# Transposing x of two batches by DMA in a fused attention and feed-forward kernel, with a new order of its steps

## The chip, the cores and the metric

The kernel runs on one core of one Trainium2 chip. A core has five engines that run side by side and wait for each other through semaphores: TensorE (PE in the profile; its weight loads are shown apart as PEld), VectorE (DVE), ScalarE (ACT), GpSimd (POOL) and SyncE (SP). SP does no arithmetic here; it starts DMA transfers, and so does POOL. The transfers of both run on the core's 16 DMA engines. The metric is the device time of the whole program in microseconds, the median of repeated runs.

## The reference

Two parts follow each other. The first is causal attention in a sliding window of 64 positions, for 8 batches of 8 heads, 576 positions and a head size of 64. The second is a feed-forward layer over all 4,608 tokens: 512 to 2,048 features, an activation h - tanh(h), and 2,048 back to 512.

```python
scores = scale * np.matmul(q, k.transpose(0, 1, 3, 2))
mask = (rel >= 0) & (rel < window)                 # rel = query position - key position, window = 64
attn = softmax(np.where(mask, scores, -1e9))
x = np.matmul(attn, v)                             # to (tokens, heads * head_dim) = (4608, 512)
h = x @ w_in                                       # 512 x 2048
out = (h - np.tanh(h)) @ w_out                     # 2048 x 512
```

## The kernel before

All matrix products are bf16 with float32 sums. The kernel is written as small Python functions, one for each kind of step, and a script (the string PLAN, line 537, played at line 621) that names the steps in the order in which they are issued. Each engine runs its own instructions in this order and waits where an operand is not ready or a buffer not free; nothing is reordered at run time. A step is written `kind.arguments`, and a last letter names the engine that does it: a ScalarE, v VectorE, p GpSimd. So the script is both a program and a schedule, and a step moved in it moves in the queue of every engine that it uses.

Attention works by pairs of heads, g = 4 * batch + pair (0 to 31), mostly two pairs at a time. The keys of the window are taken in blocks of 128 for 64 queries, nine query windows for each batch. The steps of a pair of pairs are:

- loads on POOL's queue: `qr` and `lr` bring 128 tokens of q or k of a batch (five pieces each), `LV` brings v in five pieces; for batches 0 to 2 `lk`, `lq` bring k and q of one pair in another layout, and `ck`, `cq` copy these into the order that TensorE transposes (`Fp`, `Ep`, with the copies `Fc`, `Ec` out of PSUM). From batch 3 on, `tk` and `tq` transpose k and q with DMA transposes on SP's queue (lines 171 and 179); `tz` copies the last 64 queries.
- `S` (or `Rp` for batches 0 to 2): scores on TensorE into PSUM; `Sx` (`Rx`): exp on ScalarE; `M`: the mask as a product on VectorE; `Z`, `za`, `zb`: copies of v between the two halves of the partitions.
- `PP`: probabilities times v on TensorE (line 348), with the sums of the rows as a 65th column; `DR` and three `DN` on VectorE: reciprocals, and x in token order into the tile xs (two buffers, by batch).
- x must then be turned so that features lie on partitions. `Xp` does it by TensorE (line 397, 128x128 transposes against an identity into PSUM) and `Xc` copies it into the tile xT; `Y` does it by DMA transposes on SP's queue (line 416), straight from xs to xT. In the kernel before, batches 0 to 3 go by `Xp`, batches 4 to 7 by `Y`.

The feed-forward layer works by chunks c of 512 tokens, nine in all, while a batch has 576, so a batch fills one chunk and the beginning of the next. xT has three buffers, by chunk.

- `H.c.m`: the first layer, 128 of the 2,048 hidden features (m from 0 to 15), four matmuls of 512 columns (line 431); `Hp.c.m.half` is the same in two halves (line 508), where half h needs only that half of x (half 0 comes from pairs 0 and 1 of the batch, half 1 from pairs 2 and 3).
- `A`: tanh on ScalarE (line 439) from PSUM; `G`: h - tanh(h) on VectorE (line 445) into gT. From chunk 2 on the sums of `H` alternate between two PSUM banks, so `H` of an m waits for `G` of the m that had the bank before.
- `W.c.s.part`: the second layer for 128 tokens, four matmuls of 512 columns (line 474), all in PSUM bank 2 for most chunks; `O.c.s`: the copy out of PSUM on ScalarE or VectorE and the output DMA on SP.

A buffer in use is a wait in the queue of whoever wants to write it. `LV` of batch b needs the `PP` steps of batch b - 2, and `qr` and `lr` of batch b need the DMA transposes `tq` and `tk` that read the same piece of batch b - 2. Such a wait on POOL or SP holds everything behind it in that queue.

Of the kernel before, what the change touches and what calls it, by code (L numbers as in the profile page):

```python
# [650 lines left out]
```

## Time and profile before

The time before is 307.63 us, the median of three runs (307.45 to 307.67). The profiled execution has a span of 305.2 us from its first to its last instruction; no time of its own is shown beside that, and the 2.4 us between the span and the median lie before and after it.

| | busy us | share of the span | instructions |
|---|---|---|---|
| TensorE, matmuls | 297.8 | 98% | 2599 |
| TensorE, weight loads (beside matmuls) | 149.4 | 49% | 2632 |
| VectorE | 176.2 | 58% | 316 |
| ScalarE | 157.5 | 52% | 265 |
| GpSimd (mostly issuing loads) | 103.7 | 34% | 141 |

The views used below are: the page (busy shares, the span in 40 slices, the chain of work that ended last), the groups of instructions by line and shape, the waits of an engine, the instructions in order of time, and the DMA issues with their times to landing. Within a row of the time view, the first number is the start, the second the length, and a bracket gives the idle time before it and who ended it. A matmul's length includes its way through the pipeline, so the cost of a matmul in a stream is read from one start to the next, not from its length.

### The profile page before, as it was taken

What the parts mean: (1) busy time and instruction counts of PE and PEld (TensorE: products, weight loads), DVE (VectorE), ACT (ScalarE), POOL (GpSimd) and SP (SyncE); (2) the same over time, 40 slices, a digit from 0 to 9 for tenths busy, and PEclk for the clock granted to TensorE, in tenths of its full rate; (3) what the DMA queues carried; (4) which work ended last, traced back from release to release, by engine and by line L of the source; (5) the groups of instructions that cost most, each with busy time, mean ns of one, the idle gap of its engine ahead of it and who ended that gap; (6) DMA issues with size and microseconds to landing.
All of it is one profiled execution on the core that took longest, in us unless ns stands there. A gap on an engine that the chain in (4) does not pass through costs nothing.

```text
span 305.2 us, 6469 instructions
## 1 busy us (share of the span) xinstructions
PE 297.8 (98%) x2599; PEld 149.4 (49%) x2632; DVE 176.2 (58%) x316; ACT 157.5 (52%) x265; POOL 103.7 (34%) x141
## 2 busy tenths in 40 slices
PE   8999999999999999999999999999999999999995
...
DMA  9999999995999999949999999560143010001112
GB/s 155 159 195 193 195 207 180 159 205 102 102 143 127 173 125 181 182 108 131 164 177 127 135 173 142 95 143 35 37 76 74 0 69 37 34 34 37 52 51 104
DMA packets 132878, 36.77 MB, mean 120 GB/s; under 512 B 119920, under 2 KB 127344, under 8 KB 132848
## 3 DMA queue, kind: packets, MB, share of 16 engines
q0 software_dynamic: 92752, 18.06, 85.3%
...
## 4 chain that ended last, share of the span: by engine, by line
PE 87%; DVE 5%; ACT 3%; issue 2%; POOL 2%; DVEq 0%; ACTq 0%; POOLq 0%
PE ps L474 38%; PE ps L431 30%; PE ps L508 6%; PE ps L348 3%; PE ps L304 2%; DVE gT L445 2%; PE ps L397 1%; ACT th L439 1%; PE ps L286 1%; PE ps L467 1%; DVE pt L323 1%; PE ps L260 1%; PE ps L281 1%; PE ps L227 1%; POOL qall L110 1%
## 5 line engine op out<-in xcount | busy, mean ns | idle before, releaser
L445 DVE TENSOR_TENSOR gT<-ps,th 128x512 bf16<-128x512 f32 x144 | 97.2, 687 | 85.3 <-ACT th L439 84.6
L474 PE MATMUL ps<-w_out_sb,gT 128*128 128x512 bf16 x527 | 131.5, 380 | 2.2 <-issue 0.8
L439 ACT ACTIVATE th<-ps 128x512 f32<-128x512 f32 x144 | 84.7, 599 | 93.0 <-PE ps L431 79.7
L431 PE MATMUL ps<-xT,wi 128*128 128x512 bf16 x496 | 120.7, 380 | 0.1
L474 PEld LDWEIGHTS <-gT 128*128 128x128 bf16 x560 | 53.3, 98 | 61.4
L431 PEld LDWEIGHTS <-wi 128*128 128x128 bf16 x496 | 47.0, 98 | 54.3
L145 POOL DMA_DIRECT2D vw<-in_v_dram x35 | 30.0, 872 | 36.1 <-PE ps L348 33.5
L90 ACT ACTIVATE ysb<-ps 128x512 f32<-128x512 f32 (+1 forms) x24 | 14.2, 593 | 30.9 <-PE ps L474 30.2
L166 POOL DMA_DIRECT2D qall<-in_q_dram x25 | 21.7, 881 | 24.1 <-DMA qw<-qall 21.4
L166 POOL DMA_DIRECT2D kall<-in_k_dram x25 | 21.7, 875 | 10.4 <-DMA kw<-kall 4.8
L314 ACT ACTIVATE pt<-ps 128x1024 bf16<-128x1024 f32 (+1 forms) x30 | 23.3, 816 | 3.5 <-PE ps L304 3.2
L323 DVE TENSOR_TENSOR pt<-pt,ps 128x1152 bf16<-128x1152 bf16 x28 | 20.5, 749 | 5.1 <-ACT pt L314 3.2
L508 PE MATMUL ps<-xT,wi 128*128 128x512 bf16 x80 | 20.8, 380 | 0.0
L92 DVE COPY ysb<-ps 128x512 f32<-128x512 f32 (+1 forms) x11 | 7.1, 650 | 20.5 <-PE ps L467 13.2
L368 DVE TENSOR_TENSOR xs<-ps,rcp 128x384 bf16<-128x384 f32 x28 | 15.2, 550 | 0.3
L318 ACT ACTIVATE pt<-ps 128x640 bf16<-128x640 f32 (+1 forms) x24 | 14.7, 659 | 0.8 <-PE ps L286 0.8
L348 PEld LDWEIGHTS <-pt 128*64 128x64 bf16 x504 | 9.4, 112 | 6.3 <-DVE pt L323 2.1
L90 ACT ACTIVATE kt<-ps 128x576 bf16<-128x576 bf16 x10 | 6.5, 647 | 10.8 <-PE ps L256 6.8
L227 PE MATMUL ps<-warm 128*128 128x512 bf16 (+1 forms) x35 | 10.6, 435 | 1.1 <-DVE warm L207 1.1
L508 PEld LDWEIGHTS <-wi 128*128 128x128 bf16 x80 | 7.4, 98 | 8.5 <-issue 0.4
L348 PE MATMUL ps<-vw,pt 128*64 128x65 bf16 x504 | 11.0, 197 | 0.3 <-DVE pt L323 0.2
L365 DVE TENSOR_TENSOR xs<-ps,rcp 128x384 bf16<-128x384 f32 x14 | 7.7, 550 | 0.1
...
## 6 DMA issues: line engine op xcount, KB each, us to landing
...
vw<-in_v_dram POOLq DMA_DIRECT2D x28, 128.0 KB, 6.6
qall<-in_q_dram POOLq DMA_DIRECT2D x20, 128.0 KB, 7.5
kall<-in_k_dram POOLq DMA_DIRECT2D x20, 128.0 KB, 6.8
...
```

The source lines that it names most:

```text
L90: nc.scalar.activation(o, i, ACT.Copy)
L145: nc.gpsimd.dma_start(out=w[:, 2 * i + 1, :, 0:D] if i < NF else w[64:128, 2 * i, :, 0:D], in_=v[b, :, 128 * i:128 * i + n].rearrange("h p ...
L166: nc.gpsimd.dma_start(out=token_rows(b, n)[0:c, i], in_=(q if n == "q" else k)[b, :, 128 * i:128 * i + c].rearrange("h p d -> p h d"))
L314: nc.scalar.activation(o, sp, ACT.Exp, scale=scale)
L323: nc.vector.tensor_tensor(p, p, mask.unsqueeze(1).to_broadcast([128, 2 * NJ, 64]), ALU.mult)
L348: nc.tensor.matmul(ps[r, bank, 65 * i:65 * i + 65], PT[(g + r2) % NPT][:, j, r], vw[b % 2][:, j, p0 + r2 + NP * h, :], start=True, stop=True)
L368: nc.vector.tensor_tensor(xs[b % 2][:, p0 // 2, 0:6, n // 2, :], ov[:, :, 0:D], sums[g][:, n].to_broadcast([128, 6, D]), ALU.mult)
L431: nc.tensor.matmul(hp, w_in_tile(ki, m), chunk_tile(c)[:, n.start // 64:n.stop // 64, ki % 2, 64 * (ki // 2):64 * (ki // 2) + 64], start=( ...
L439: nc.scalar.activation(th[:, n], hp, ACT.Tanh)
L445: nc.vector.tensor_tensor(gT[c][:, m, columns(s)], hp, th, ALU.subtract)
L474: nc.tensor.matmul(yp, gT[c][:, m, s * 128:(s + 1) * 128], w_out_sb[:, m, :], start=n == 1 and i == 0, stop=n == 4 and i == 3)
L508: nc.tensor.matmul(hp, w_in_tile(half + 2 * i, m), chunk_tile(c)[:, :, half, 64 * i:64 * i + 64], start=n == 1 and i == 0, stop=n == 2 and ...
```

## The change

Nothing is changed in the functions; the script gets a new text from step `Ep.8` on, just before chunk 0's last first-layer steps H.0.14, H.0.13 and H.0.15. The 16 steps `Xp` and `Xc` of batches 2 and 3 are gone (8 each, 36 TensorE transposes), and in their place stand `Y.2.0`, `Y.2.1`, `Y.3.0` and `Y.3.1`, eight more DMA transposes on SP's queue (each batch's half lies in two chunks, so each step issues two). All other steps stay, in a new order, and some get another engine or PSUM bank: `ck.9` and `cq.11` from ScalarE and VectorE to GpSimd, `zb.1.3` from GpSimd to ScalarE, `za.1.2` from VectorE to ScalarE and `za.1.3` the other way, `tz.3` and `tz.7` to GpSimd, and several output copies between ScalarE and VectorE. The attention of batches 3 to 7 stands earlier in the script. In the diff below the first part of both texts is shown, to the attention of batch 4.

```diff
@@ the script PLAN, from line 553 on
-    cq.8.v G.0.9 G.0.10 Rp.7.1.3 A.0.11 wo.2 Fc.8.7.a G.0.11 Rp.7.0.5 H.0.12 lk.9.p Rx.7.0.5 A.0.12 Ep.8.1
-    Rx.7.1.3 cq.9.v H.0.14 M.4 wo.3 zb.1.3.p G.0.12 Ec.8.1.a PP.4 wo.1 A.0.14 H.0.15 mk DR.4 DN.4.1 G.0.14
-    A.0.15 H.0.13 DN.4.0 za.1.3.a W.0.0.0 Rp.8.0.3 G.0.15 A.0.13 Rp.8.1.5 DN.4.2 zb.1.2.a za.1.2.v Rx.8.1.5
-    W.0.1.0 M.7 qr.3.3 LV.2.3 lk.11.p PP.6 Rx.8.0.3 Xp.1.0.1.3 W.0.0.2 G.0.13 Xp.1.0.0.4 DR.6 Xc.1.0.1.3.a
-    DN.6.2 DN.6.0 W.0.1.2 DN.6.1 Xp.1.1.0.5 lk.10.p ck.9.a Xc.1.0.0.4.a Fp.9.3 Xc.1.1.0.5.a Xp.1.1.1.4
-    lr.3.2 lq.10.p lq.11.p LV.2.2 Hp.1.0.0 Ep.9.7 Xc.1.1.1.4.v Ec.9.7.a Fc.9.3.a Hp.1.0.1 W.0.1.3 W.0.0.3
-    qr.3.4 LV.2.0 Rp.9.1.5 Rp.9.0.3 LV.2.1 W.0.0.1 O.0.0.a M.8 LV.2.4 W.0.1.1 lr.3.1 lr.3.4 A.1.0 tq.3.4
-    G.1.0 O.0.1.a Rx.9.1.5 Rx.9.0.3 ck.11.a M.9 ck.10.a W.0.2.1 W.0.2.0 W.0.2.3 W.0.2.2 W.0.3.2 qr.3.1
-    O.0.2.a Fp.11.5 cq.10.v W.0.3.1 W.0.3.3 Hp.1.1.1 W.0.3.0 Fp.10.7 Ep.10.3 Hp.1.1.0 O.0.3.v Ec.10.3.v
-    Hp.1.2.1 Hp.1.2.0 Fc.10.7.a A.1.1 A.1.2 Rp.10.1.3 G.1.1 cq.11.v G.1.2 Fc.11.5.a H.1.3 Ep.11.6 tk.3.2
-    A.1.3 Rx.10.1.3 H.1.4 A.1.4 G.1.3 Ec.11.6.a H.1.5 A.1.5 qr.3.0 Z.2 H.1.6 qr.3.2 PP.8 G.1.5 Rp.11.0.3
-    A.1.6 tk.3.1 tq.3.3 lr.3.0 H.1.8 Rx.11.0.3 G.1.4 G.1.6 DR.8 H.1.7 DN.8.2 A.1.8 A.1.7 H.1.9 tq.3.1 G.1.8
-    H.1.11 G.1.7 A.1.9 tk.3.4 H.1.10 lr.3.3 A.1.11 A.1.10 DN.8.1 G.1.9 Rp.11.1.3 Rx.11.1.3 Rp.10.0.6 tq.3.2
-    G.1.11 DN.8.0 G.1.10 Rx.10.0.6 H.1.12 tq.3.0 M.10 H.1.14 A.1.12 M.11 H.1.13 Xp.2.0.1.3 Xp.2.0.0.4 G.1.12
-    A.1.13 A.1.14 Xc.2.0.1.3.a PP.10 H.1.15 LV.4.1 LV.3.1 A.1.15 Xc.2.0.0.4.a LV.3.3 G.1.13 LV.3.2 LV.3.0
-    DR.10 DN.10.1 DN.10.0 tk.3.0 DN.10.2 tk.3.3 LV.3.4 LV.4.0 G.1.14 lr.4.2 qr.4.0 lr.4.1 lr.4.0 qr.5.3
-    LV.4.2 W.1.0.1 W.1.0.2 Xp.2.1.1.6 W.1.0.0 G.1.15 qr.4.1 lr.4.4 Xp.2.1.0.5 Xc.2.1.0.5.a W.1.0.3
-    Xc.2.1.1.6.v qr.4.3 lr.4.3 H.2.3 Hp.2.0.0 Hp.2.0.1 tk.4.4 O.1.0.a A.2.3 LV.4.3 qr.4.4 LV.4.4 A.2.0
-    W.1.1.2 G.2.3 Hp.2.1.0 tz.3.a Hp.2.1.1 W.1.1.3 G.2.0 qr.4.2 qr.5.4 lr.5.2 H.2.2 A.2.1 G.2.1 S.12 A.2.2
-    G.2.2 H.2.5 Sx.12.2 Sx.12.0 W.1.1.1 Z.3 W.1.1.0 A.2.5 Sx.12.1 O.1.1.a tk.4.1 tq.4.0 M.12 tk.4.0 H.2.4
-    M.13 tk.4.3 tq.4.4 G.2.5 A.2.4 PP.12 W.1.2.3 H.2.7 lr.6.4 lr.5.4 DR.12 DN.12.2 G.2.4 tq.4.3 tk.4.2
-    tq.4.1 lr.6.3 DN.12.0 A.2.7 lr.5.3 lr.5.1 lr.5.0 tq.4.2 DN.12.1 H.2.6 G.2.7 qr.5.2 S.14 H.2.9 A.2.6
-    Sx.14.2 Sx.14.1 A.2.9 tk.5.4 Sx.14.0 G.2.6 G.2.9 M.14 M.15 qr.6.0 W.1.2.0 H.2.8 W.1.2.1 W.1.2.2
-    Xp.3.0.1.3 A.2.8 G.2.8 tq.5.3 H.2.11 O.1.2.v PP.14 DR.14 H.2.10 A.2.11 A.2.10 Xc.3.0.1.3.v G.2.10
-    Xp.3.0.0.4 W.1.3.2 G.2.11 tq.5.4 W.1.3.3 H.2.12 A.2.12 H.2.13 Z.4 A.2.13 W.1.3.1 G.2.12 G.2.13 H.2.14
-    W.1.3.0 H.2.15 DN.14.2 O.1.3.a DN.14.1 A.2.15 A.2.14 DN.14.0 Xp.3.1.0.6 W.2.0.1 Xp.3.1.1.7 W.2.0.0
-    G.2.14 W.2.0.2 Xc.3.1.1.7.v Xc.3.0.0.4.a Xc.3.1.0.6.a G.2.15 qr.5.0 Hp.3.0.0 W.2.0.3 Hp.3.1.1 Hp.3.1.0
-    O.2.0.a A.3.1 W.2.1.1 Hp.3.0.1 W.2.1.2 G.3.1 tz.4.v A.3.0 S.16 Sx.16.2 W.2.1.3 Sx.16.1 G.3.0 H.3.3
-    W.2.1.0 M.17 Sx.16.0 M.16 H.3.2 A.3.3 PP.16 G.3.3 O.2.1.a A.3.2 tk.5.2 qr.5.1 qr.6.4 H.3.5 LV.5.3
-    W.2.2.1 DR.16 A.3.5 tk.5.1 DN.16.2 tq.5.2 G.3.2 DN.16.1 H.3.4 DN.16.0 Y.4.0 A.3.4 S.18 G.3.5 W.2.2.0
...
+    cq.8.v G.0.9 G.0.10 Rp.7.1.3 A.0.11 wo.2 Fc.8.7.a G.0.11 Rp.7.0.5 H.0.12 lk.9.p Rx.7.0.5 A.0.12 Ep.8.7
+    Rx.7.1.3 cq.9.v H.0.14 M.4 G.0.12 Ec.8.7.a A.0.14 H.0.13 wo.3 H.0.15 M.7 G.0.14 LV.2.0 wo.1 qr.3.1
+    lk.10.p ck.9.p qr.3.0 lq.11.p lk.11.p lq.10.p LV.2.3 qr.3.2 lr.3.0 qr.3.4 cq.11.p LV.2.1 LV.2.2 LV.2.4
+    PP.4 Rp.8.0.3 W.0.0.0 A.0.13 A.0.15 za.1.3.v zb.1.3.a Rx.8.0.3 za.1.2.a Rp.8.1.3 Rx.8.1.3 zb.1.2.a DR.4
+    G.0.15 DN.4.0 DN.4.2 DN.4.1 W.0.1.0 Ep.9.4 G.0.13 Xp.1.0.0.3 PP.6 Xp.1.0.1.1 W.0.1.2 Xc.1.0.0.3.v
+    Xc.1.0.1.1.a DR.6 DN.6.2 DN.6.1 W.0.0.2 Fp.9.6 Hp.1.0.0 DN.6.0 Xp.1.1.0.5 Xp.1.1.1.3 Xc.1.1.1.3.v
+    Ec.9.4.v Xc.1.1.0.5.a Fc.9.6.a W.0.0.3 W.0.1.3 Rp.9.1.6 Rp.9.0.3 Hp.1.0.1 W.0.0.1 W.0.1.1 O.0.0.a
+    Rx.9.1.6 A.1.0 O.0.1.a tk.3.0 tq.3.1 lr.3.2 lr.3.3 lr.3.4 tk.3.2 ck.10.a cq.10.a W.0.2.3 W.0.2.1 W.0.2.2
+    W.0.2.0 W.0.3.0 G.1.0 ck.11.v M.8 lr.3.1 tk.3.3 tq.3.2 tk.3.4 tk.3.1 tq.3.0 qr.3.3 LV.3.3 tq.3.3 LV.3.1
+    LV.3.0 LV.3.2 Ep.11.6 Ep.10.1 Ec.10.1.v O.0.2.a Rx.9.0.3 M.9 W.0.3.1 W.0.3.2 Fp.11.5 Fp.10.4 W.0.3.3
+    Hp.1.1.1 Hp.1.1.0 O.0.3.a Fc.10.4.v Ec.11.6.v Fc.11.5.a A.1.1 G.1.1 H.1.3 Hp.1.2.1 Rp.11.1.3 Rp.10.0.5
+    Hp.1.2.0 H.1.4 A.1.3 Rx.10.0.5 Rx.11.1.3 A.1.2 G.1.3 Z.2 G.1.2 H.1.6 Rp.10.1.3 PP.8 A.1.4 A.1.6
+    Rx.10.1.3 G.1.4 H.1.5 H.1.7 A.1.5 A.1.7 DR.8 G.1.6 M.10 G.1.5 DN.8.0 G.1.7 H.1.9 A.1.9 G.1.9 H.1.8 A.1.8
+    G.1.8 DN.8.1 Rp.11.0.3 H.1.10 A.1.10 Rx.11.0.3 H.1.12 H.1.11 A.1.12 A.1.11 G.1.10 DN.8.2 M.11 H.1.13
+    PP.10 G.1.12 G.1.11 H.1.15 A.1.13 tq.3.4 tz.3.p qr.5.4 qr.4.4 LV.3.4 lr.4.4 lr.4.0 lr.4.2 lr.4.3 qr.4.1
+    qr.4.2 lr.4.1 qr.5.0 qr.5.2 qr.4.0 qr.4.3 Y.2.0 H.1.14 A.1.15 A.1.14 G.1.13 DR.10 DN.10.2 DN.10.0
+    DN.10.1 G.1.14 G.1.15 mk Y.2.1 W.1.0.0 W.1.0.2 W.1.0.1 W.1.0.3 S.12 Hp.2.0.0 Sx.12.1 Sx.12.2 Sx.12.0
+    O.1.0.v W.1.1.1 W.1.1.2 Hp.2.0.1 Hp.2.1.1 Hp.2.1.0 W.1.1.3 A.2.0 A.2.1 Z.3 M.12 G.2.0 G.2.1 M.13 H.2.2
+    H.2.3 PP.12 A.2.2 G.2.2 A.2.3 H.2.4 A.2.4 G.2.3 DR.12 DN.12.0 G.2.4 DN.12.1 DN.12.2 W.1.1.0 H.2.5 tq.4.4
+    tk.4.2 Y.3.0 tk.4.4 tq.4.2 tk.4.3 tk.4.0 H.2.6 S.14 O.1.1.a A.2.5 A.2.6 G.2.6 G.2.5 W.1.2.1 W.1.2.2
+    H.2.10 tk.4.1 tq.4.3 tq.4.0 tq.4.1 H.2.11 W.1.2.3 W.1.2.0 Sx.14.1 Sx.14.2 tz.4.a Sx.14.0 A.2.11 A.2.10
+    G.2.11 G.2.10 M.14 H.2.13 H.2.8 O.1.2.v M.15 A.2.13 A.2.8 G.2.13 G.2.8 W.1.3.3 W.1.3.1 H.2.7 H.2.12
+    A.2.12 A.2.7 W.1.3.2 W.1.3.0 PP.14 G.2.12 G.2.7 DR.14 DN.14.0 DN.14.2 DN.14.1 O.1.3.a H.2.15 A.2.15
+    Y.3.1 qr.5.1 LV.4.3 LV.4.0 qr.5.3 qr.6.1 LV.4.4 LV.4.1 LV.5.0 lr.5.1 lr.6.3 lr.5.4 lr.5.2 LV.4.2 LV.5.1
+    lr.6.1 qr.6.0 LV.5.2 lr.5.3 lr.5.0 qr.6.3 LV.5.4 qr.6.4 tk.5.2 tk.5.1 tk.5.4 tq.5.4 G.2.15 W.2.0.0
+    H.2.14 H.2.9 A.2.14 A.2.9 S.16 G.2.9 W.2.0.1 W.2.0.2 G.2.14 W.2.0.3 Sx.16.2 Sx.16.0 Sx.16.1 M.17 O.2.0.v
+    M.16 Hp.3.0.1 Hp.3.0.0 Hp.3.1.1 W.2.1.0 Hp.3.1.0 A.3.0 G.3.0 A.3.1 G.3.1 W.2.1.2 W.2.1.3 H.3.2 W.2.1.1
+    H.3.3 A.3.2 G.3.2 O.2.1.a A.3.3 G.3.3 H.3.4 A.3.4 W.2.2.3 W.2.2.2 H.3.7 W.2.2.0 G.3.4 Z.4 PP.16 DR.16
+    A.3.7 H.3.6 W.2.2.1 G.3.7 DN.16.0 DN.16.1 DN.16.2 A.3.6 O.2.2.a G.3.6 H.3.5 S.18 A.3.5 G.3.5 H.3.8 A.3.8
+    Sx.18.2 Sx.18.0 Sx.18.1 G.3.8 M.18 M.19 W.2.3.2 H.3.9 W.2.3.1 W.2.3.0 A.3.9 G.3.9 H.3.10 PP.18 H.3.11
...
+    W.8.2.0 W.8.2.2 W.8.2.3 W.8.2.1 W.8.3.3 O.8.2.v O.9.0.a W.8.3.0 W.8.3.1 O.8.3.v"""
```

73 lines of the change are left out of this document (35 added, 38 removed).

## The prediction

> **What bounds the kernel now.** I read the page first (busy shares, slices, chain), then the waits of TensorE, then the groups by line, and last the time view around the steps that move.
>
> ```profile
> span 305.2 us, 6469 instructions
> PE 297.8 (98%) x2599; PEld 149.4 (49%) x2632; DVE 176.2 (58%) x316; ACT 157.5 (52%) x265; POOL 103.7 (34%) x141
> PE   8999999999999999999999999999999999999995
> DMA  9999999995999999949999999560143010001112
> PE 87%; DVE 5%; ACT 3%; issue 2%; POOL 2%; DVEq 0%; ACTq 0%; POOLq 0%
> ```
>
> TensorE is busy in every slice from the second to the last but one, and 87% of the chain that ended last is its own work. The DMA engines are full until about slice 28 (214 us).
>
> ```profile
> PE ps L227 <- DVE warm L207: 1.1, 1, 1.1
> PE ps L474 <- issue: 0.8, 5, 0.2
> PE ps L348 <- DVE pt L323: 0.2, 1, 0.2
> PEld L348 <- DVE pt L323: 2.1, 5, 0.5
> ```
>
> The matmuls themselves hardly wait; the weight loads ahead of the probabilities-times-v products (PP) wait 2.1 us, of which most is hidden under the matmul still running. So the end is set by how much TensorE has to do plus what it waits, and every term below is a sum on TensorE's queue.
>
> **What is removed.** 36 of 72 transposes (Xp), and their copies out of PSUM (Xc).
>
> ```profile
> L397 PE MATMUL ps<-ident,xs 128*128 128x128 bf16 x72 | 6.3, 220 | 0.0
> 44.39 0.45 PE L397 MATMUL ps<-ident,xs 128*128 128x128 bf16 x5
> 44.68 0.38 PE L474 MATMUL ps<-w_out_sb,gT 128*128 128x512 bf16 x1
> L90 ACT ACTIVATE xT<-ps 128x512 bf16<-128x512 bf16 x7 | 4.1, 600 | 2.2 <-PE ps L397 2.2
> ```
>
> Five transposes start at 44.39 and the next matmul at 44.68: 0.29 / 5 = 58 ns each, so 36 x 58 ns = 2.1 us leave TensorE. The 220 ns in the group's row is the length through the pipeline and is not what one costs in a stream. "TensorE: Matmul & The Clock Gate" in the Trainium skill (Part 4: PE-mode transpose) gives about 275 ns for such a transpose in one kernel; by that figure 9.9 us would leave, an estimate from that page, and the row above contradicts it. The copies are worth nothing directly: ScalarE is 52% and VectorE 58% busy; at the full 0.6 us each in a stretch where one of them is the bound, they are counted there.
>
> Old waits go as well, because the steps around them move. Their bounds are 0.2 (the matmuls' own row) and 2.1 us (the weight loads' row); I take 0.6, nearer the matmuls' row, since a weight load runs ahead of its matmul.
>
> **What is added: waits in the new order.** TensorE blocks are counted from these rows: four matmuls of H or W 0.86 us, a PP 0.70, a score block S 0.79 (from 85.75 to 86.54), a transpose of q or k (Ep) 0.25 (60.30 to 60.55), two score groups Rp issued together 0.37 (71.48 to 71.85), alone about half of it and a change of shape, 0.3.
>
> ```profile
> 245.73 0.86 PE ps L474 x4
> 100.23 0.70 PE ps L348 x35
> 85.75 0.22 PE L299 MATMUL ps<-q,kw 128*128 128x64 bf16 x2
> 86.54 1.04 PE L431 MATMUL ps<-xT,wi 128*128 128x512 bf16 x4
> 60.30 0.42 PE L260 MATMUL ps<-ident,qb 96*128 96x96 bf16 x6
> 60.55 1.46 PE L508 MATMUL ps<-xT,wi 128*128 128x512 bf16 x6
> 71.48 0.43 PE L286 MATMUL ps<-qp,kt 64*128 64x64 bf16 x18
> 71.85 2.77 PE L431 MATMUL ps<-xT,wi 128*128 128x512 bf16 x12
> ```
>
> (1) Around PP.6. In the new order ScalarE has, from the end of H.0.15 to PP.6, a tanh, zb.1.3, an exp, za.1.2, an exp and zb.1.2, and PP.6 needs the last.
>
> ```profile
> 41.08 0.64 ACT L90 ACTIVATE vw<-vw 64x520 bf16<-64x520 bf16 x1
> 41.62 0.57 ACT L439 ACTIVATE th<-ps 128x512 f32<-128x512 f32 x1
> 42.90 1.19 ACT L318 ACTIVATE pt<-ps 128x512 bf16<-128x512 f32 x2
> ```
>
> That is 0.6 + 3 x 0.64 + 2 x 0.6 and 0.2 to start, 3.9 us. TensorE has PP.4, two Rp, two W, Ep.9 and an Xp of four: 0.70 + 0.6 + 1.72 + 0.25 + 0.23 = 3.5; the second Rp waits for the first's exp and hides some of this. So it waits about +0.4. The pads mk (two memsets) and the output copies that changed engine cost nothing while the 0.86 us blocks between their producer and user cover them; without that cover each would cost its 0.3 to 0.7 us once.
>
> (2) From PP.8 to PP.10.
>
> ```profile
> 66.00:75.00 9.00, 8.94 (x106) 4.72 (x105) 8.55 (x16) 6.21 (x11) 0.00 (x0) 1.00 0.93 130
> 100.00:110.00 10.00, 9.95 (x86) 5.08 (x86) 6.19 (x13) 3.93 (x7) 5.42 (x7) 1.00 1.27 147
> 110.00:120.00 10.00, 9.79 (x82) 5.02 (x83) 4.71 (x9) 5.76 (x11) 4.51 (x6) 1.00 2.31 158
> 66.11 0.76 PE L348 MATMUL ps<-vw,pt 128*64 128x65 bf16 x36
> 75.05 0.77 PE L348 MATMUL ps<-vw,pt 128*64 128x65 bf16 x36
> ```
>
> VectorE is busy for 8.55 of the first nine us, with fourteen of its sixteen instructions between the two products (eight G, two M, DR and three DN), about 8.5. TensorE took 8.94 from PP.8 to PP.10. In the new order it has the same eight H, but neither the nine transposes (0.52) nor the two score groups (0.37): 8.05. VectorE has the same fourteen, and starts about 0.2 ahead, since Z.2 no longer ends right at PP.8. So PP.10 waits 8.5 - 0.2 - 8.05 = about +0.3; bounds 0 and 0.6. The transposes of batch 2 that went here were partly cover for VectorE.
>
> (3) x of batches 2 and 3, now by DMA.
>
> ```profile
> L416 SPq DMA_TRANSPOSE xT<-xs x16: 1120/1238/2263, 124.8 to 229.4; - x16
> DMA to landing us min/median/max: 2.3/3.7/8.2
> 163.31 0.27 DVE L356 RECIPROCAL rcp<-ps 128x18 f32<-128x18 f32 x1 [0.60 <-PE ps L348]
> 164.05 0.54 DVE L368 TENSOR_TENSOR xs<-ps,rcp 128x384 bf16<-128x384 f32 x1
> 164.51 0.55 DVE L365 TENSOR_TENSOR xs<-ps,rcp 128x384 bf16<-128x384 f32 x1
> 163.41 4.18 POOL L145 DMA_DIRECT2D vw<-in_v_dram  x5 [18.06 <-PE ps L348]
> vw<-in_v_dram POOLq DMA_DIRECT2D x6, 128.0 KB, 8.2
> xT<-xs SPq DMA_TRANSPOSE x4, 5.2
> 174.37 1.89 PE L508 MATMUL ps<-xT,wi 128*128 128x512 bf16 x8
> ```
>
> The last four rows are batch 5: as PP.22 ends, POOL's loads of v are let go, and in the stretch from 160 to 176 us the x transposes take 5.2 us from issue to landing (median), 8.2 at most, against 2.3 undisturbed. Their first user stood at 174.37, 11 us after the product. The new order leaves less. From PP.14's end to Hp.3.0.1 TensorE has seven blocks and S.16: 7 x 0.86 + 0.79 = 6.8. VectorE needs 0.2 to start, 0.27, and three DN of 0.46 to 0.55: 2.0 to the issue of Y.3.1. A landing of up to 4.8 us is free. POOL by then waits in front of qr.6.1 for tq.4.1 to land, some 1.5 us before Y.3.1 is issued, so a burst like batch 5's is under way: between 2.3 (no wait) and 8.2 (3.4 us) I take 5.3, +0.5. For Y.2.1 the way from PP.10's end to Hp.2.0.1 is eight blocks, S.12 and half a block, 8.1, and VectorE still has two G ahead of DR: 3.0, so 5.1 is free; POOL is issuing batch 4's loads. Between 0 and 3.1 I take +0.4. The first halves (Y.2.0, Y.3.0) have 3 us more and are covered.
>
> (4) The queues past which steps moved.
>
> ```profile
> POOL qall L166 <- DMA qw<-qall: 21.4, 1, 21.4
> POOL kall L166 <- DMA kw<-kall: 4.8, 1, 4.8
> ```
>
> SP: Y.3.0 waits for DN.12 with seven tq and tk of batch 4 behind it. From PP.12's end: 3.4 to the last DN, ten transposes at 1.24 and one output (0.4) = 16.2 to the end of tq.4.1's issue, landed 1.1 later (2.3 less the issue), 17.3. S.16, which needs it, is 20.5 us of TensorE's blocks after PP.12: covered by 3.2. POOL: qr.6.1 may not overwrite what tq.4.1 reads (the same kind of wait cost POOL 21.4 us once), and behind it stand eight loads, LV.4.2 the last, at 0.84 each (4.18 / 5) and 8.2 to land: 17.3 + 6.7 + 8.2 = 32.2. Z.4 must start 33.7 after PP.12's end for PP.16 to be in time: covered by 1.5 us, and PP.16 waits for what comes later than that. ck.9 and cq.11 on POOL wait for their loads with LV.2.1, LV.2.2 and LV.2.4 behind them; cq.11 stands 11 us of TensorE's blocks before PP.8's Z.2 at the least, and three loads and a landing are 2.5 + 8.2: just covered. tz.3 on POOL waits for tq.3.4 with LV.3.4 third behind it; tq.3.4 is the last of SP's eleven for batch 3 and ends by PP.10, from which Z.3 is 7 us: covered by 1. Together +0.2 for what of this runs out, between 0 and 3.
>
> (5) Two small ones: W.1.3.3 behind M.14 and O.1.2 on VectorE +0.1, H.2.9 behind three DN and G.2.15 +0.1.
>
> **The sum.** Of the profiled execution's span: 305.2 - 2.1 - 0.6 + 0.4 + 0.3 + 0.5 + 0.4 + 0.2 + 0.2 = 304.5. The median of the runs is 2.4 above the span, so 306.9 us against 307.63, 0.2% less. A measurement of this kernel can tell about 0.2% (0.6 us) from no change, so this stands on the edge: below 307.0 counts as faster, above 308.2 as slower.
>
> **The rivals.**
>
> Clean: every new wait is covered and the whole 2.7 us is won: 304.9. For it speaks that the matmuls waited hardly at all in the order before; against it, (1) and (2) are sums of busy time, not of latencies. By a rule in the Trainium skill, "DMA: Bandwidth & Descriptors", Queues, rings and completion order, a DMA engine goes round its queues packet by packet, so SP's transposes would not stand behind POOL's backlog; by that rule (3) costs nothing and the sum is 306.0. The landings of 5.2 and 8.2 beside a POOL burst speak against it.
>
> Late x (slower): one mechanism, Y.3.1 landing behind the burst that tq.4.1 releases on POOL. At the longest landing, 8.2, Hp.3.0.1 waits 3.4 instead of 0.5: 309.8. It decides from a landing of about 6.7 us (a wait of 1.9 and 308.3). For it: 5.2 is a median and 8.2 was reached in just this stretch of batch 5. Against: the burst starts only 1.5 us before.
>
> Covered: the removed transposes were cover for VectorE and ScalarE in both batches, not only in (2), so that half of the 2.1 us and the old waits' 0.6 come back as small waits, 1.7, of which (1) and (2) hold 0.7: 306.9 + 1.0 = 307.9, no change. For it: VectorE's 8.55 of 9; against: in 100 to 120 us, where batch 3's stood, it is busy 6.19 and 4.71 of ten (the two rows above).
>
> The 275 ns transposes: 304.5 - 7.8 + 2.4 = 299.1; the 58 ns row excludes it nearly.
>
> **How the numbers follow.** The forecast (306.2 to 307.6) has 0.40, clean 0.16, covered (307.3 to 308.2) 0.15, late x and its like (above 308.2) 0.28, the 275 ns 0.01. Of the forecast's case 0.24 lies below 307.0. Faster: 0.24 + 0.16 + 0.01 = 0.41; slower 0.28; the same 0.31. The range 304.9 to 309.3 leaves out 0.01, a little of clean and the upper half of late x, 0.17 in all; the forecast's own range is 306.2 to 307.6.
>
> **What the profile after would show.** L397 has 36 matmuls instead of 72, and L416 24 transposes instead of 16. In (1) TensorE's PP at about 44 us starts after a ScalarE copy of v, in (2) PP.10's weight load is released by VectorE's M (L323). In (3) the L508 group at about 112 us starts after a landing of xT, with a gap before it. If that gap is above 2 us the forecast is wrong, and late x holds; if gaps are nowhere, clean holds; if S.16 or PP.16 waits for a DMA, (4) was taken too low.

## The result and the profile after

The changed kernel takes 310.52 us (median of five runs, 309.73 to 311.74), against 307.67 for the kernel before beside it: a ratio of 1.0086, interval 1.0059 to 1.0113. It is 0.9% slower; forecast were 306.9 us and a range of 304.9 to 309.3. The profiled run is the fastest of the five, 309.73 us with a span of 308.0.

The page of the changed kernel, the lines that answer to those of before:

```profile
span 308.0 us, 6442 instructions
PE 299.0 (97%) x2596; PEld 147.6 (48%) x2596; DVE 175.0 (57%) x309; ACT 154.0 (50%) x257; POOL 106.0 (34%) x144
PE   8999999999999989999999799999999999999996
DMA  9999999999999999999999999441032010001012
PE 78%; DMA 9%; POOL 4%; issue 3%; DVE 2%; SPq 2%; ACT 1%; POOLq 0%; DVEq 0%
```

Two slices of TensorE are no longer full, the 15th (108 to 115 us) and the 23rd (169 to 177 us). In the chain that ended last TensorE's share has fallen from 87% to 78%, and DMA, which was not in it at all, has 9%. The same loss in the view by stretches, where the number after PE is TensorE's busy time in the 80 us from 100 to 180 us, first after and then before:

```profile
sum 80.00, PE 76.13 PEld 36.98 DVE 45.56 ACT 37.27 POOL 33.04; mean PE 19.03 PEld 9.24 DVE 11.39 ACT 9.32 POOL 8.26
```

```profile
sum 80.00, PE 79.06 PEld 39.43 DVE 47.62 ACT 40.42 POOL 33.48; mean PE 19.76 PEld 9.86 DVE 11.91 ACT 10.10 POOL 8.37
```

Nearly 3 us of TensorE's busy time are lost there. The loss is larger when it is read from starts, since a matmul's length runs on into the wait behind it. TensorE's instructions in order of time in the changed kernel show the five places (start, length, and in the bracket the wait and what ended it):

```profile
108.55 0.22 PE L299 MATMUL ps<-q,kw 128*128 128x64 bf16 x2
109.53 0.23 PE L304 MATMUL ps<-qw,kw 64*128 64x64 bf16 x4 [0.76 <-DMA qw<-qall]
109.96 0.62 PE L304 MATMUL ps<-qw,kw 64*128 64x64 bf16 x30 [0.20 <-DMA qw<-qall]
110.52 2.76 PE L474 MATMUL ps<-w_out_sb,gT 128*128 128x512 bf16 x12
...
123.48 1.03 PE L474 MATMUL ps<-w_out_sb,gT 128*128 128x512 bf16 x4
124.95 0.76 PE L348 MATMUL ps<-vw,pt 128*64 128x65 bf16 x36 [0.45 <-DVE vw L152]
...
141.93 1.03 PE L474 MATMUL ps<-w_out_sb,gT 128*128 128x512 bf16 x4
143.39 0.22 PE L299 MATMUL ps<-q,kw 128*128 128x64 bf16 x2 [0.44 <-DMA kw<-kall]
...
168.83 1.24 PE L474 MATMUL ps<-w_out_sb,gT 128*128 128x512 bf16 x5
171.01 1.89 PE L431 MATMUL ps<-xT,wi 128*128 128x512 bf16 x8 [0.94 <-DVE gT L445]
172.73 1.03 PE L474 MATMUL ps<-w_out_sb,gT 128*128 128x512 bf16 x4
174.85 0.23 PE L299 MATMUL ps<-q,kw 128*128 128x64 bf16 x2 [1.09 <-DMA kw<-kall]
```

From one start to the next, less what the blocks take in a stream (S 0.79, four matmuls 0.86): S.16 loses 1.97 - 0.79 = 1.2, PP.16 1.47 - 0.86 = 0.6, S.20 1.46 - 0.86 = 0.6, H.4.13 2.18 - 5 x 0.216 = 1.1, S.24 2.12 - 0.86 = 1.3. Together 4.8 us. 305.2 - 2.1 for the transposes + 4.8 = 307.9, and the span is 308.0; the small terms of the prediction are taken up below. The two that wait for VectorE (PP.16, H.4.13) wait for landings behind it: VectorE's copies of v (Z.4) stood after a load, and the subtraction of H.4.13 stood behind tz.6, which waited for a DMA transpose of batch 6.

What the chain of the changed kernel holds of DMA tells where it comes from (start and length of each piece):

```profile
104.50 5.42 DMA qw<-qall
113.72 2.35 POOL kall L166 x3
118.72 4.47 DMA kall<-in_k_dram
140.76 2.50 DMA kw<-kall
158.24 10.62 DMA kall<-in_k_dram
168.88 5.92 DMA kw<-kall
```

It is one thread. Batch 4's last transpose tq.4.1 lands at 109.92 and lets S.16 go, and POOL with it. POOL then issues the loads that stood behind, and the copies of v ahead of PP.16 wait until 123.2 for one of them (the chain names the load of k issued at 118.72; by the landings it is LV.4.2, issued at 117.00). Batch 5's k is among these loads, so batch 5's transposes begin at 122.17, and their last one, tk.5.3 (140.76), is what S.20 waits for, and POOL too, which stood at lr.7.3. The load of k of batch 6 at 158.24 then takes 10.6 us beside the loads and transposes that were let go with it, and the transpose behind it, issued at 168.88, holds S.24. SP's and POOL's own rows at the thread's beginning:

```profile
91.26 2.59 SPq L416 DMA_TRANSPOSE xT<-xs  x2
...
101.88 5.66 SPq L179 DMA_TRANSPOSE qw<-qall  x3
...
108.73 2.69 SPq L416 DMA_TRANSPOSE xT<-xs  x2
122.17 3.89 SPq L171 DMA_TRANSPOSE kw<-kall  x3
```

```profile
94.64 1.00 POOL L166 DMA_DIRECT2D qall<-in_q_dram  x1
110.45 0.88 POOL L166 DMA_DIRECT2D qall<-in_q_dram  x1 [14.81 <-DMA qw<-qall]
```

POOL stands 14.8 us at qr.6.1, and SP has nothing to issue from 111.4 to 122.2, since the pieces of k that it needs are behind that wait.

The change itself did what it says: in the rows of line 397 and line 416, 36 transposes are left on TensorE and 24 are on SP.

```profile
L397 PE MATMUL ps<-ident,xs x36: 217/219/230, 20.3 to 48.6; 128*128 128x128 bf16 x36
L416 SPq DMA_TRANSPOSE xT<-xs x24: 1142/1225/1718, 76.5 to 230.5; - x24
DMA to landing us min/median/max: 2.2/3.6/7.4
```

### The profile page after: what moved, and what is told of

It reads as the page before. It is cut to its first block, busy times and chain, and to the rows that moved or that the text cites. A ratio compares the mean times of both kernels' runs of the same rounds, so it can differ in the third digit from the quotient of the medians.

```text
span 308.0 us, 6442 instructions
## 1 busy us (share of the span) xinstructions
PE 299.0 (97%) x2596; PEld 147.6 (48%) x2596; DVE 175.0 (57%) x309; ACT 154.0 (50%) x257; POOL 106.0 (34%) x144
## 4 chain that ended last, share of the span: by engine, by line
PE 78%; DMA 9%; POOL 4%; issue 3%; DVE 2%; SPq 2%; ACT 1%; POOLq 0%; DVEq 0%
PE ps L474 32%; PE ps L431 29%; PE ps L508 5%; DMA kall<-in_k_dram 5%; DMA kw<-kall 3%; PE ps L348 2%; PE ps L304 2%; DMA qw<-qall 2%; PE ps L260 1%; PE ps L286 1%; POOL vw L145 1%; PE ps L467 1%; PE ps L281 1%; POOL kall L166 1%; PE ps L227 1%
## 5 line engine op out<-in xcount | busy, mean ns | idle before, releaser
L474 PE MATMUL ps<-w_out_sb,gT 128*128 128x512 bf16 x560 | 133.9, 379 | 0.0
L90 ACT ACTIVATE ysb<-ps 128x512 f32<-128x512 f32 (+1 forms) x25 | 14.8, 593 | 32.1 <-PE ps L474 27.9
L166 POOL DMA_DIRECT2D qall<-in_q_dram x25 | 22.5, 919 | 17.1 <-DMA qw<-qall 14.8
L368 DVE TENSOR_TENSOR xs<-ps,rcp 128x384 bf16<-128x384 f32 x28 | 15.0, 550 | 0.2
L318 ACT ACTIVATE pt<-ps 128x640 bf16<-128x640 f32 (+1 forms) x24 | 14.8, 653 | 0.6 <-PE ps L286 0.5
L92 POOL COPY q<-qw 64x256 bf16<-64x256 bf16 x2 | 0.8, 398 | 27.1 <-DMA qw<-qall 27.1
L92 DVE COPY qp<-ps 128x576 bf16<-128x576 bf16 x6 | 4.5, 742 | 9.0 <-PE ps L256 6.8
```

The lines of the kernel that those rows point to most:

```text
L90: nc.scalar.activation(o, i, ACT.Copy)
L166: nc.gpsimd.dma_start(out=token_rows(b, n)[0:c, i], in_=(q if n == "q" else k)[b, :, 128 * i:128 * i + c].rearrange("h p d -> p h d"))
L368: nc.vector.tensor_tensor(xs[b % 2][:, p0 // 2, 0:6, n // 2, :], ov[:, :, 0:D], sums[g][:, n].to_broadcast([128, 6, D]), ALU.mult)
L474: nc.tensor.matmul(yp, gT[c][:, m, s * 128:(s + 1) * 128], w_out_sb[:, m, :], start=n == 1 and i == 0, stop=n == 4 and i == 3)
```

## The experiments

Eighteen kernels, each timed beside the kernel before. The ratios with their intervals:

| kernel | median us | ratio to before | interval |
|---|---|---|---|
| the changed kernel | 310.52 | 1.0086 | 1.0059 to 1.0113 |
| s1: transposes by DMA in the old order | 323.92 | 1.0512 | 1.0460 to 1.0564 |
| e4: new order, batches 2 and 3 on TensorE | 310.48 | 1.0083 | 1.0055 to 1.0111 |
| k1: new order, batch 2 by DMA, 3 on TensorE | 309.25 | 1.0049 | 1.0022 to 1.0076 |
| k2: k1 with local moves | 308.19 | 1.0027 | 0.9993 to 1.0061 |
| e1: qr.6.1 later | 314.37 | 1.0219 | 1.0181 to 1.0256 |
| e2: Y.3.0 later | 309.74 | 1.0061 | 1.0032 to 1.0089 |
| e3: e1 and e2 | 314.09 | 1.0208 | 1.0168 to 1.0247 |
| g1: tq.3.4 earlier | 313.21 | 1.0166 | 1.0113 to 1.0219 |
| h1: old order to PP.16, then new | 308.54 | 1.0039 | 1.0015 to 1.0063 |
| h2: new order to PP.16, then old | 316.74 | 1.0307 | 1.0264 to 1.0349 |
| f1: k of batch 6 earlier | 311.63 | 1.0125 | 1.0075 to 1.0174 |
| f2: new order, an eighth of v | 305.30 | 0.9922 | 0.9901 to 0.9942 |
| c1: old order, an eighth of v | 307.29 | 0.9977 | 0.9960 to 0.9995 |
| g2: k of batch 5 earlier | 309.26 | 1.0051 | 1.0021 to 1.0080 |
| g3: scores later on TensorE | 309.26 | 1.0055 | 1.0020 to 1.0090 |
| g4: g2 and g3 | 309.08 | 1.0036 | 1.0019 to 1.0053 |
| g5: g3 and three more local moves | 309.52 | 1.0050 | 1.0024 to 1.0077 |
| g6: g5 and W.1.1.0 earlier | 309.77 | 1.0051 | 1.0016 to 1.0085 |

All edits are edits of the script, except f2 and c1. The changed kernel has five runs, the others four to twelve. Where an interval overlaps the changed kernel's, as those of e2, e4, f1, h1, g2, g3, g5, g6, k1 and k2 do, the gains and losses told below are differences of medians and not shown beyond them.

### Places in the queues: e1, e2, e3

My first theory was that two places cost: qr.6.1 in POOL's queue and Y.3.0 in SP's. The rival was the traffic, wherever it stands.

```diff
 e1
-qr.5.3 qr.6.1 LV.4.4 LV.4.1 LV.5.0 lr.5.1 lr.6.3 lr.5.4 lr.5.2 LV.4.2 LV.5.1 lr.6.1
+qr.5.3 LV.4.4 LV.4.1 LV.5.0 lr.5.1 lr.6.3 lr.5.4 lr.5.2 LV.4.2 LV.5.1 qr.6.1 lr.6.1
 e2
-tq.4.4 tk.4.2 Y.3.0 tk.4.4 tq.4.2 tk.4.3 tk.4.0 ... tk.4.1 tq.4.3 tq.4.0 tq.4.1
+tq.4.4 tk.4.2 tk.4.4 tq.4.2 tk.4.3 tk.4.0 ... tk.4.1 tq.4.3 tq.4.0 tq.4.1 Y.3.0
```

> The order after, with one load (qr.6.1) moved eight places back in POOL's queue, behind batch 5's first k loads; nothing else. Theory A (places in the queues): qr.6.1 held POOL for 14.8 us until the transpose that reads its buffer had landed, and the waits of PP.16 (0.5 us), S.20 (0.55) and of H.4.13 with S.24 (2.4) are its late consequence; S.16's own wait of 1.2 us comes from SP's queue and stays. So 310.5 - 3.4 = 307.1 us, 306.3 to 308.0. Theory B (traffic): eight more transposes on DMA engines that are full until slice 27 make everything land later, wherever it stands; moving one load only moves the wait: 309.5 to 311.5.

> The order after, with Y.3.0 moved in SP's queue from the third to the twelfth place of its row, behind the transposes of batch 4; nothing else. Theory A: batch 4's last transpose is issued 3.6 us earlier (two transposes and the wait for DN.12 no longer stand ahead), S.16's 1.2 us go and POOL is let go about 3.6 us earlier, so that PP.16's 0.5 and S.20's 0.55 go too and some of the 2.4 us of batch 6 stays: 307.5 us, 306.5 to 309. Theory B: as many packets as before, so 309.5 to 311.5.

> Both moves together. Theory A: all five waits go, 310.5 - 4.8 = 305.7 us, 305.0 to 306.5, faster than before. Theory B: 309 or more.

e1 went the wrong way for both theories: 314.4 us, 3.9 more than the changed kernel. TensorE's wait in S.16, a stretch of that wait (the 0.50 is the granted clock, as a share of full speed), the matmuls behind it, and the DMA issues from 96 to 112 us with their median times to landing, beside the same stretch of the changed kernel:

```profile
PE ps L304 <- DMA qw<-qall: 5.0, 2, 3.1
112.00:114.00 2.00, 0.00 (x0) 0.00 (x0) 0.00 (x0) 0.00 (x0) 0.00 (x0) 0.50 2.09 199
115.30 4.36 PE L474 MATMUL ps<-w_out_sb,gT 128*128 128x512 bf16 x12
119.49 1.46 PE L508 MATMUL ps<-xT,wi 128*128 128x512 bf16 x6
```

```profile
kw<-kall SPq DMA_TRANSPOSE x3, 8.1
qw<-qall SPq DMA_TRANSPOSE x4, 8.0
xT<-xs SPq DMA_TRANSPOSE x2, 7.7
```

```profile
kw<-kall SPq DMA_TRANSPOSE x3, 7.5
qw<-qall SPq DMA_TRANSPOSE x4, 6.7
xT<-xs SPq DMA_TRANSPOSE x2, 3.5
```

With POOL free, its loads run beside batch 4's last transposes and Y.3.1. Those take 8.0 and 7.7 us instead of 6.7 and 3.5, and S.16 waits 5 us instead of 1. Behind this wait comes a second loss: the granted clock is 0.50 from about 112 to 118 us, the twelve matmuls at 115.30 take 4.19 us from start to start where the changed kernel's take 2.60 (110.52 to 113.12), and the 30 score products ahead of them 0.94 instead of 0.56, some 2.0 us in all. So the wait at qr.6.1 was no mere loss: it kept the loads away from transposes that TensorE was about to need. In e2 the move did what was expected at its place, S.16 no longer waits; but x of batch 3 now lands late (in its profile Hp.3.0.1 waited 1.2 us for it), and 0.8 us are left of the 3 expected. e3 is as slow as e1 (314.1); in its profile it is mostly x that TensorE waits for, 3.8 us in two waits.

### Which part of the change: s1, e4, h1, h2

s1 puts the four steps Y into the old order in the places of Xp and Xc; e4 puts Xp and Xc into the new order in the place of Y.

```diff
 s1 (the order before)
-Xp.2.0.1.3 Xp.2.0.0.4 ... Xp.2.1.1.6 W.1.0.0 ... Xp.3.0.1.3 ... Xp.3.1.0.6 (and all Xc.2, Xc.3)
+Y.2.0                 ... Y.2.1 W.1.0.0      ... Y.3.0      ... Y.3.1
 e4 (the order after)
-H.1.15 ... Y.2.0 ... Y.2.1 W.1.0.0 W.1.0.2 W.1.0.1 ... Y.3.0 ... W.1.3.3 ... Y.3.1 ... H.2.14
+H.1.15 Xp.2.0.0.3 Xp.2.0.1.4 ... W.1.0.0 W.1.0.2 Xp.2.1.0.3 Xp.2.1.1.4 W.1.0.1 ...
+W.1.3.3 Xp.3.0.0.3 Xp.3.0.1.4 ... H.2.14 Xp.3.1.0.3 Xp.3.1.1.4 (each with its Xc behind it)
```

> The order before, in which only the 36 transposes and eight copies of batches 2 and 3 are replaced, in their places, by Y.2.0, Y.2.1, Y.3.0 and Y.3.1. Theory H (the old order has no room for a landing): x of batch 2 is needed 1.5 us after the last product of it, and lands some 7 us after; batch 3 the same with the burst of 106 to 114 us beside it. So 2.1 us less on TensorE against some 5.5 and 6 us of waits: 317 us, 312 to 320. Rival I (the loss of the change lies in the new order alone, and the transposes by DMA are a plain gain): 305.5 to 307.

> The order after, but batches 2 and 3 transposed on TensorE again (36 transposes, eight copies out of PSUM), so without the four steps Y. Theory A: 36 x 58 ns = 2.1 us more on TensorE, and S.16 and POOL let go as early as in the run with Y.3.0 moved, or a little earlier: 307.5 + 2.1 = 309.6 us, 308 to 311. Theory B: the DMA engines carry what they carried before, all 4.9 us of waits go and 2.1 come back: 307.7 us, 307 to 308.3.

s1 takes 323.9 us, 16 more than before, and its waits are the landings of x:

```profile
PE ps L431 <- DMA xT<-xs: 7.1, 1, 7.1
PE ps L508 <- DMA xT<-xs: 6.8, 2, 4.1
```

The forecast for this, 317 us (312 to 320), was too low: the waits are 13.9 us instead of some 11.5, and behind each long one the granted clock falls to 0.50, so that the eleven matmuls from 87.72 to 92.18 us take 4.46 us, where a stream takes 0.216 each, 2.38. The old order has no room for a transpose by DMA, where it has room for nine transposes on TensorE (0.5 us) and a copy. The new order makes that room: in the changed kernel's profile the users of x wait 0.1 us at most. But e4 takes as long as the changed kernel (310.48), with 2.1 us more work on TensorE and no Y of these batches in SP's queue. Its profile has 0.8 us at W.1.0.2, a wait for VectorE that the changed kernel doesn't have and which comes from a copy Xc that I put on ScalarE ahead of a tanh; the rest of its 2.7 us over before is put down to the order. So the new order by itself, with TensorE's work as before, is slower by some 2 us (0.9 to 2.6 by the interval), and the transposes by DMA, set into it, save their work and cost about as much in waits. The profile of e4, one of its faster runs (308.85), shows where each belongs: S.16, PP.16, S.20 and H.4.13 wait for nothing in it, so in that run those four waits are gone with the eight transposes, and only S.24 waits, 1.1 us.

h1 and h2 cut the two orders at PP.16 and play the first part of one and then the steps that are left in the order of the other. In h2 the cut lies between H.3.7 and its tanh, so that one hidden tile of 144 is formed from the sums of H.3.5, which share its PSUM bank; the work is the same.

> The order before up to PP.16 (with its 36 transposes on TensorE), and from there the steps that are left in the order after. Theory C (the early part): the waits of batches 5 and 6 are late consequences of what is lost up to PP.16, so here they don't come: 307.8 us, 307.2 to 308.4. Theory D (the late part): the order after PP.16 holds POOL on lr.7.3 with batch 6's loads behind it, and S.24 and H.4.13 wait here too, 1.3 to 2.4 us: 309.6, 308.6 to 310.5.

> The reverse: the order after up to PP.16 (x of batches 2 and 3 by DMA), and from there the steps that are left in the order before. Theory C: S.20, H.4.13 and S.24 wait as in the order after, about 2.9 us in all: 310.3, 309.3 to 311.5. Theory D: only S.16 and PP.16 wait, 1.7 us, which the 2.1 us less on TensorE pay: 307.5 us, 306.8 to 308.3.

h1 is 1.2 us slower than before (0.5 to 1.9): the late part has a loss of its own, less than D had (its profile has 0.8 us at S.24 and 0.7 at a block that waits for VectorE), and the rest of the 2.9 is put down to what is ahead of PP.16. h2 is worse than either theory allowed, 316.7: behind the new early part batch 5 is not yet loaded, and the old late part has no room for that. Each late part fits its own early part, so the cut measures the fit too, and I take only h1's sign from it.

### Earlier loads: f1, g1, g2

```diff
 f1
-LV.6.2 lr.7.3 lr.7.1 qr.7.4 qr.6.2 qr.7.3 lr.6.2 qr.7.2 LV.6.3 qr.7.1 lr.6.0 ... LV.6.4 lr.6.4
+LV.6.2 lr.6.0 lr.6.2 lr.6.4 lr.7.3 lr.7.1 qr.7.4 qr.6.2 qr.7.3 qr.7.2 LV.6.3 qr.7.1 ... LV.6.4
 g1
-tk.3.0 tq.3.1 lr.3.2 ... PP.10 G.1.12 G.1.11 H.1.15 A.1.13 tq.3.4 tz.3.p qr.5.4
+tk.3.0 tq.3.1 tq.3.4 lr.3.2 ... PP.10 G.1.12 G.1.11 H.1.15 A.1.13 tz.3.p qr.5.4
 g2
-Y.3.1 qr.5.1 LV.4.3 LV.4.0 qr.5.3 qr.6.1 LV.4.4 LV.4.1 LV.5.0 lr.5.1 lr.6.3 lr.5.4 lr.5.2 LV.4.2
+Y.3.1 lr.5.2 lr.5.1 lr.5.4 lr.5.0 qr.6.1 LV.4.3 LV.4.0 LV.4.4 LV.4.1 LV.4.2 qr.5.1 qr.5.3 LV.5.0 lr.6.3
```

> The order after, with three loads of k of batch 6 (lr.6.0, lr.6.2, lr.6.4) moved in POOL's queue ahead of lr.7.3, which holds POOL until batch 5's last transpose of k has landed. Theory D: S.24 and H.4.13 no longer wait: 310.5 - 2.4 = 308.1 us, 307.3 to 309. Theory C: these loads meet batch 5's transposes instead, and S.20 waits for what S.24 no longer does: 309.7 to 311.5.

> The order after, with one DMA transpose (tq.3.4) moved forward in SP's queue from the last to the third place of batch 3's row. In the order after, POOL stands from 64.8 to 80.2 us at tz.3 and qr.5.4 until tq.3.4 has landed; here it lands at about 68, and batch 4's loads begin 12 us earlier. Theory E (POOL's late start): S.16 and PP.16 no longer wait, nor does S.20: 310.5 - 2.2 = 308.3 us, 307.3 to 309.3. Theory F (what meets in the DMA engines): the loads now run beside batch 3's last transposes and Y.2, so S.12 and Hp.2.1.1 wait 2 us or more in their place: 310.5 to 313.

> The order after, with four loads of k of batch 5 put ahead of qr.6.1 in POOL's queue in the place of four others (two of q, two of v), which go behind it; as many loads as before beside batch 4's transposes. Theory G (batch 5 starts late, since its k stands behind qr.6.1): SP can start batch 5 at about 113 instead of 122 us, so S.20 (0.55), H.4.13 and S.24 (2.4) no longer wait, while S.16's 1.2 stays: 307.6 us, 306.7 to 308.6. Against it, if the DMA engines have no room between 110 and 140 us: 309.5 to 311.5.

f1 takes 311.6: S.24 no longer waited, but H.4.13 still did (0.9 us), and S.20 lost 2.3 us, as C had it. g1 takes 313.2: S.16 no longer waited, but the first products of chunk 2 waited for x of batch 2 (3.6 us by TensorE's waits), as F had it; behind the longer of these waits, 3.3 us, the granted clock fell to 0.50 once more. Only g2, which puts no more loads beside the transposes than there were, gained by the medians: 309.3, 1.3 us of the 2.9 expected. Loads that come earlier are paid for by transposes that land later.

### The traffic: f2, c1

The loads of v of batches 4 to 7 bring one head of eight, in both orders.

```diff
+        hs = H if b < 4 else 1
-        nc.gpsimd.dma_start(out=w[:, 2 * i + 1, :, 0:D] if i < NF else w[64:128, 2 * i, :, 0:D],
-                            in_=v[b, :, 128 * i:128 * i + n].rearrange("h p d -> p h d"))
+        nc.gpsimd.dma_start(out=w[:, 2 * i + 1, 0:hs, 0:D] if i < NF else w[64:128, 2 * i, 0:hs, 0:D],
+                            in_=v[b, 0:hs, 128 * i:128 * i + n].rearrange("h p d -> p h d"))
```

> The order after with every instruction in its place, but the 20 loads of v of batches 4 to 7 bring one head instead of eight (so those batches are computed with other values of v); that takes 2.1 MB of 18 MB off POOL's queue. Theory B' (landings: the transposes land late because the engines are full of loads): S.16, S.20, S.24, H.4.13 and PP.16 wait together for at most 1.5 us instead of 4.7: 307 us, 305.5 to 308. Against it, if the order in which the queues are held sets the waits, S.16 and S.24 wait as before: 309.5 to 311.

> The order before, with the loads of v of batches 4 to 7 cut to one head of eight (so those batches are computed with other values of v), as in the run of the order after with one head of v. Theory B' (the new order waits on landings, the old one doesn't): 307.2 us, 306.6 to 307.9. If fewer bytes help any order: 305.5 or less, and the 5.2 us that the order after gained say little of the change.

The new order falls to 305.3 us, by 5.2; the old one by 0.5, to 307.3. With every instruction in its place, all five waits are gone from the new order. One new wait stands in its profile, 1.0 us for x of batch 2.

So the five waits are waits for landings, and hang on how much is loaded beside the transposes. It doesn't single out the bytes: the shorter loads also take POOL less time to issue. And it shows what the change would bring if DMA had room: with so much less to load it is faster than the old order under the same cut by 2.0 us (by the ratios 1.7), about the 2.1 us of the transposes.

### Local covers: g3 to g6, k1, k2

If a score block waits 1 us for a landing and has 6 to 14 us before its product, it can stand a block later.

```diff
 g3
-S.16 G.2.9 W.2.0.1 W.2.0.2 ... S.20 G.3.12 Z.5 G.3.15 W.3.0.3 ... S.24 W.4.0.1 W.4.0.3
+G.2.9 W.2.0.1 W.2.0.2 S.16 ... G.3.12 Z.5 G.3.15 W.3.0.3 S.20 ... W.4.0.1 W.4.0.3 S.24
-tz.6.v DR.22 ... A.4.13 Z.6 G.4.13 G.4.14 W.4.0.0
+DR.22 ... A.4.13 Z.6 G.4.13 G.4.14 tz.6.v W.4.0.0
 g5: g3 with S.16 behind W.2.0.1, and
-M.17 O.2.0.v ... Sx.20.1 Sx.20.0 A.4.0 ... A.4.1
+O.2.0.v M.17 ... A.4.0 ... A.4.1 Sx.20.1 Sx.20.0
 g6: g5, and
-W.1.1.2 Hp.2.0.1 ... DN.12.2 W.1.1.0 H.2.5
+W.1.1.2 W.1.1.0 Hp.2.0.1 ... DN.12.2 H.2.5
```

(S.20 stands one block later in g3, not four.)

> The order after, with queues of SP and POOL as they are; on TensorE S.16 stands two blocks later, S.20 four and S.24 two, and VectorE's copy tz.6, which waits for a landing, stands behind the G that TensorE waits for. If the waits are local (a product placed 1 to 2 us ahead of its landing, with 6 to 14 us of cover behind it): 4.1 us less, 306.4 us, 305.7 to 307.5. If the landings are late for what follows too (PP.16, PP.20, PP.24 and POOL's next loads): 308.5 to 310.5.

> The four loads of k and the later scores together. If both are as theory G and the local waits have it: 305.8 us, 305.2 to 306.8, faster than before. If either only moves the waits: 307.5 to 310.

> The order after with the queues of SP and POOL as they are; S.16 and S.20 one block later on TensorE, S.24 two, tz.6 behind the G that TensorE waits for, the output copy O.2.0 ahead of the masks of batch 4, and two exps of S.20 behind A.4.1. The profile of the run with later scores shows what is to go: 1.4 us at W.2.1.0, 0.3 at W.2.0.2, 0.5 at H.4.3. If those are all: 309.3 - 2.2 = 307.1 us, 306.3 to 308. If the waits come back at other places, since the landings vary from run to run: 308.3 to 309.8.

> As the last, and W.1.1.0 moved ahead of Hp.2.0.1, so that x of batch 2 has 0.86 us more to land (Hp.2.1.1 waited 0.7 us in the run with later scores). 0.6 us less than the last: 306.5 us, 305.7 to 307.5; no difference, if H.2.5 then waits for its G.

g3 won 1.3 us of the 4.1, and its profile names a new wait, TensorE's for an output copy that stood on VectorE behind the later masks:

```profile
115.54 1.02 PE L474 MATMUL ps<-w_out_sb,gT 128*128 128x512 bf16 x4 [1.43 <-DVE ysb L92]
```

g5 takes that away, and is no faster (309.5); the waits come back elsewhere, in its profiled run at PP.16 (1.8 us, for VectorE's copies of v) and for x (1.3 us).

The ten runs of g5 lie between 307.2 and 312.9 us, while 25 of the kernel before beside it lie between 307.1 and 309.5. A profile shows one of these runs; mending the waits of that one doesn't mend the next. g4 and g6 can't be told from g3 and g5, but g4's interval (1.0019 to 1.0053) is the only one of this group that lies clear of the changed kernel's.

k1 puts batch 3 alone back on TensorE, where e4 has both, and k2 adds g5's moves.

> The order after, with batch 2's x by DMA as there and batch 3's x back on TensorE (18 transposes, four copies). Theory J (batch 3's half of the change costs more than it saves, since its transposes stand in SP's queue among batch 4's): 1.05 us more on TensorE, S.16's 1.2 and PP.16's 0.5 go, S.20's 0.55 partly: 309.4 us, 308.5 to 310.3. If the new order itself is what costs: 310.5 to 311.5.

> The same with the local moves (S.16, S.20, S.24, tz.6, O.2.0 and two exps). The local moves gave 1 us to the order after; with J's 1.1 that is 308.4 us, 307.3 to 309.4. Faster than before (below 307.1) only if batch 6's waits go too, 1 in 10.

Both came out some 0.2 us from the forecast: 309.25 and 308.19. By the medians batch 3's half of the change costs 1.3 us more than it saves, and batch 2's half wins about what it saves in work (e4 to k1, 1.2 us); the intervals of the three kernels overlap, so these are sizes to go by and not to rely on. k2 can't be told from the kernel before (0.9993 to 1.0061). No version that does the whole work beats it.

## Why the prediction was wrong

By its own steps:

- **What is removed** was right: 36 transposes are gone, and f2 and c1 differ by 1.7 to 2.0 us, about what was put down for them (2.1). The old waits, put down at 0.6, no run measures by themselves: the weight loads' row for VectorE's masks fell from 2.1 us to 0.4, most of it hidden before. With the 0.6 and the 0.4 of (1) the balance of the span would be 307.7 instead of 307.9; 308.0 doesn't decide between them.
- **(1)** was right in kind: forecast 0.4, and the changed kernel lost 0.2 (the bracket) at the second Rp and, from 44.36 to 44.78 for four transposes of 58 ns, 0.2 at PP.6.

```profile
42.97 0.29 PE L286 MATMUL ps<-qp,kt 64*128 64x64 bf16 x8 [0.16 <-ACT pt L318]
...
44.36 0.39 PE L397 MATMUL ps<-ident,xs 128*128 128x128 bf16 x4
44.78 0.77 PE L348 MATMUL ps<-vw,pt 128*64 128x65 bf16 x36
...
72.76 1.46 PE L431 MATMUL ps<-xT,wi 128*128 128x512 bf16 x6
74.15 0.77 PE L348 MATMUL ps<-vw,pt 128*64 128x65 bf16 x36
...
113.12 1.46 PE L508 MATMUL ps<-xT,wi 128*128 128x512 bf16 x6
```

- **(2)** was not there: six matmuls of H ahead of PP.10 take 1.39 us against 1.30. Forecast 0.3, measured below 0.1. The two small waits of **(5)**, forecast 0.2, were not there either.
- **(3)** was not there in this run either: Hp.3.0.1 follows at 113.12 without a wait. Forecast 0.5 and 0.4. The reason is not the one that I weighed. POOL's burst did not meet Y.3.1, since qr.6.1 held POOL until 110.45, 1.7 us after Y.3.1's first issue; and S.16's own wait ahead of it gave 1.2 us more. Where loads do run beside it (e1), x takes 7.7 us, near the 8.2 that bounded the term.
- **(4)** is the step that failed: forecast 0.2 with a bound of 3, measured 4.8. It failed twice. First, its landing: I let tq.4.1 land 13.9 us after Y.3.0's issue (ten transposes at 1.24 us, an output and an undisturbed landing), and called S.16 covered by 3.2. It landed 109.92 - 91.26 = 18.7 after: the last transpose's issue ended at 107.54 instead of 12.8 us after 91.26, which is 104.1, and the landing came 2.4 us after that instead of 1.1. I had quoted 5.2 and 8.2 us for landings beside a burst of loads, and used them in (3), but not in (4), whose transposes run beside the loads that POOL had issued until 95.6 us; the last of these, qr.5.3 at 94.64, took 14.2 us to land. Second, its end: I followed the late landing to PP.16 and stopped. The wait at qr.6.1 then passed to batch 5's loads, its transposes and batch 6's, and S.20, H.4.13 and S.24, which no term of the sum named, hold 3.0 of the 4.8 us.

Times to landing follow the loads that run beside. The kernel before shows it within a few microseconds, first from 100 to 106 us, with three loads issued, and then from 108 to 112, with five:

```profile
qw<-qall SPq DMA_TRANSPOSE x3, 2.5
kw<-kall SPq DMA_TRANSPOSE x3, 3.7
```

```profile
qw<-qall SPq DMA_TRANSPOSE x3, 7.5
kw<-kall SPq DMA_TRANSPOSE x1, 7.8
```

The 6.7 and 7.5 us of batch 4's transposes in the changed kernel, quoted above beside e1, are near the second pair. Late in the changed kernel, from 180 to 205 us, with only four loads issued, both medians are 2.5.

Of the rivals, the sign belongs to the slower one, and its 309.8 is near the result by luck, since its mechanism was not seen: Y.3.1 landed in time. Clean holds for (1) to (3), nearly, and not for the queues. Covered is out: in the changed text TensorE waited for VectorE's or ScalarE's own work at no place by more than some 0.2 us.

Two readings of the prediction were off without a part in its failure. The DMA engines of the kernel before are nine tenths busy up to slice 25 (191 us), not 28. And the 2.4 us from span to time set the span of one run against the median of others; the profiled run of the changed kernel has 1.7 (309.73 less 308.0).

By the Trainium skill ("DMA: Bandwidth & Descriptors", Queues, rings and completion order) a DMA engine goes round its queues packet by packet, so that SP's transposes should not stand behind POOL's backlog. The runs don't contradict the turns, but they show that taking turns isn't free: the same two transposes of x took 3.5 us with POOL standing and 7.7 with POOL loading.

What stays open: why the landings of the new order differ so much from run to run (of the twelve runs of k2 five lie between 307.6 and 308.0 and three above 311). A part of the difference is the clock. The mean granted clock is 0.993 or 0.994 in just these three runs of k2 and at least 0.998 in the others; likewise 0.994 or 0.995 in the three slowest of e4's ten. A mean of 0.994 over 308 us is 0.006 x 308 = 1.8 us of clock lost, an estimate, on top of the wait ahead of it. It is not the whole, since g3 has runs up to 311.7 us at a clock of 1.00. Open is also what of a transpose's 7 us beside loads is the engines' time and what is waiting in SP's queue. No run separates the two.
